# SwiGLU on one core: the first w1 piece issued by three queues, one of them GpSimd's

## The chip, the cores and the metric

The kernel runs on one core of a Trainium2 chip. A core has a matrix engine (TensorE, PE in the profile), a vector engine (VectorE, DVE), an activation engine (ScalarE, ACT), GpSimd (POOL) and a sync engine (SyncE, SP), each with an instruction stream of its own. Loads and stores are started by an instruction on SP, ScalarE or GpSimd and are then moved by the core's 16 DMA engines. Engines wait for each other, and for loads, by semaphores. The metric is the device time of one execution in microseconds; the time of a kernel is the median of its runs.

## The reference

A gated feed-forward block in bf16, with 1024 tokens (32 x 32), D = 512 and F = 1792:

```python
gate = jnp.einsum("bsd,df->bsf", x, w1)
up = jnp.einsum("bsd,df->bsf", x, w3)
h = _silu(gate) * up
out = jnp.einsum("bsf,fd->bsd", h, w2)
```

## The kernel before

**Tiling.** TensorE contracts over the partition axis, 128 at a time. D is 4 slices (index `dt`), F is 14 slices (`fo`), the tokens are 8 tiles of 128 (`nt`) in 2 blocks of 512 (`nb`). gate and up are computed transposed, F on the partitions and tokens along the row, so x is needed transposed (`xT`, D on the partitions). h is kept in that form (`hT`), and serves as the weights of the third product, whose result has the tokens on its partitions and goes out in rows.

**How x gets transposed.** Three quarters of x come in by two transposing loads on SP (lines 78 and 82). The first 256 tokens (tiles 0 and 1, `x_sb`) are loaded as they are, and TensorE transposes them: 8 matmuls of 128 columns against an identity matrix `ident` (`turned`, line 104), copied from PSUM to `xT` by VectorE and ScalarE in turn (`put`, line 114). GpSimd makes `ident` with two instructions of `make_identity`, called on line 51.

**Order.** The schedule is written out by hand: every engine executes its instructions in the order of the code, and semaphores are put in by the framework. TensorE does 6 matmuls on a constant (`keep_warm`, line 92), the 8 transposes, and then the first three F slices (`FK` = 3) for the first 256 tokens: 12 gate matmuls, ordered so that all three slices use `dt` 0, then 1, 2 and 3, and 12 up matmuls in the same order. Then these slices for tokens 256 to 511, whose `xT` comes from the load of line 78. Then the other 11 slices for block 0 and all 14 for block 1, 8 matmuls of 512 columns for each, and last the third product, one token tile after the other. Behind each pair of gate and up banks ScalarE forms the sigmoid (line 131) and VectorE two products (lines 133 and 134).

**Loads.** `load_w` takes the slices `c0` to `c1` of F and `d0` to `d1` of D. The piece that TensorE needs first, w1's first three F slices (384 KB), is split in two halves of 192 KB: `dt` 0 and 1 (used by gate matmuls 1 to 6) and `dt` 2 and 3 (matmuls 7 to 12). Lines 71 to 75 put the loads on two queues. SP issues token tile 0 of x, then the first half of w1's piece; ScalarE issues token tile 1 of x, then a small activation that brings its table in, then the second half. SP goes on with the two halves of w3's first piece, the first transposing load, the larger pieces of w1 and w3, the second transposing load, and all of w2. GpSimd issues no load at all.

Of the kernel before, what the change touches and what calls it, by code (L numbers as in the profile page):

```python
# [10 lines left out]
def kernel(  # L11
# [8 lines left out]
    nc = tc.nc  # L20
# [10 lines left out]
    DT = D // P  # L31
# [7 lines left out]
    w1_v = w1.rearrange("(dt p) f -> p dt f", p=P)  # L39
# [8 lines left out]

    x_view = x_flat.rearrange("(nt p) d -> p nt d", p=P)
    ident = consts.tile([P, P], bf16, name="ident")  # L50
    make_identity(nc, ident[:])
    x_sb = consts.tile([P, HB // P, D], bf16, name="x_sb")
    xT = consts.tile([P, DT, N], bf16, name="xT")
    w1_sb = consts.tile([P, DT, F], bf16, name="w1_sb")
# [4 lines left out]
    FK = 3  # L59

    def load_x(queue, t0, t1):
        queue.dma_start(out=x_sb[:, t0:t1, :], in_=x_view[:, t0:t1, :])  # L62

    def load_w(queue, w_sb, w_v, c0, c1, d0=0, d1=DT):
        f0, f1 = c0 * P, c1 * P
        queue.dma_start(out=w_sb[:, d0:d1, f0:f1], in_=w_v[:, d0:d1, f0:f1])
# [3 lines left out]

    load_x(nc.sync, 0, 1)
    load_x(nc.scalar, 1, 2)
    load_w(nc.sync, w1_sb, w1_v, 0, FK, 0, 2)
    nc.scalar.activation(table[:], one, SIGMOID)  # L74
    load_w(nc.scalar, w1_sb, w1_v, 0, FK, 2, DT)
    load_w(nc.sync, w3_sb, w3_v, 0, FK, 0, 2)
    load_w(nc.sync, w3_sb, w3_v, 0, FK, 2, DT)
    nc.sync.dma_start_transpose(out=xT[:, :, HB:NB], in_=x_flat[HB:NB, :])
# [142 lines left out]
```

## Time and profile before

| | us |
|---|---|
| median of 11 runs | 82.29 |
| fastest and slowest of them | 81.77, 84.26 |
| the profiled execution | 84.38 |
| its span, first to last instruction | 82.6 |
| TensorE busy in the span | 78.2 (95%) |
| VectorE, ScalarE, GpSimd busy | 39.5, 23.4, 0.7 |

The profile is of one execution, and all times in it count from the start of its span. The page's list of groups gives, for each kind of instruction, its line, engine, operation, output and inputs with their shapes, the count, the busy time and the mean of one, and the idle time of the engine ahead of it with what ended that idle time. The timeline gives the same in order of time, with equal neighbours merged: start, length, engine and line, and how many. The chain of waits follows the work that ended last back to the start. A list of DMA issues gives the size of each load and the time from its issue to its landing; PEld is the loading of weights into the array, and a "q" behind an engine's name is its sequencer, which issues the DMAs.

### The profile page before, as it was taken

What the parts mean: (1) busy time and instruction counts of PE and PEld (TensorE: products, weight loads), DVE (VectorE), ACT (ScalarE), POOL (GpSimd) and SP (SyncE); (2) the same over time, 40 slices, a digit from 0 to 9 for tenths busy, and PEclk for the clock granted to TensorE, in tenths of its full rate; (3) what the DMA queues carried; (4) which work ended last, traced back from release to release, by engine and by line L of the source; (5) the groups of instructions that cost most, each with busy time, mean ns of one, the idle gap of its engine ahead of it and who ended that gap; (6) DMA issues with size and microseconds to landing.
All of it is one profiled execution on the core that took longest, in us unless ns stands there. A gap on an engine that the chain in (4) does not pass through costs nothing.

```text
span 82.6 us, 1014 instructions
## 1 busy us (share of the span) xinstructions
PE 78.2 (95%) x382; PEld 38.5 (47%) x388; DVE 39.5 (48%) x60; ACT 23.4 (28%) x40; POOL 0.7 (1%) x6
## 2 busy tenths in 40 slices
PE   6979999999999999999999999999999999999960
PEld 2446784444444444444444444444444444444550
DVE  0130069898788787887878878775000000000010
ACT  4410074224422244222442223430202211220220
POOL 3000000000000000000000000000000000000000
PEclk9999999999999999999999999999999999999999
DMA  1999999999900000000000000000011011011012
GB/s 24 299 253 300 339 349 347 307 229 373 333 29 0 0 0 0 0 0 0 0 12 0 0 0 0 0 4 0 0 64 64 0 64 64 8 64 64 10 54 64
DMA packets 10789, 7.67 MB, mean 93 GB/s; under 512 B 3616, under 2 KB 10784, under 8 KB 10784
## 3 DMA queue, kind: packets, MB, share of 16 engines
q1 hardware_dynamic: 10368, 7.28, 30.4%
q10 hardware_dynamic: 416, 0.33, 1.2%
q8 instruction: 3, 0.05, 0.2%
q14 instruction: 2, 0.02, 0.1%
HBM read 5.77 MB, written 1.05 MB: 83 GB/s over the span
## 4 chain that ended last, share of the span: by engine, by line
PE 90%; DMA 5%; issue 1%; SPq 0%; DVE 0%; DVEq 0%
PE gate_ps L121 31%; PE up_ps L121 30%; PE o_ps L174 29%; DMA w_sb<-in_w_dram 5%; SPq L62 0%; DVE o_sb L183 0%; DVEq L183 0%
## 5 line engine op out<-in xcount | busy, mean ns | idle before, releaser
L121 PEld LDWEIGHTS <-w_sb 128*128 128x128 bf16 x248 | 25.2, 102 | 25.8 <-DMA w_sb<-in_w_dram 0.9
L121 PE MATMUL gate_ps<-xT,w_sb 128*128 128x512 bf16 (+1 forms) x122 | 29.9, 372 | 0.7 <-DMA w_sb<-in_w_dram 0.6
L121 PE MATMUL up_ps<-xT,w_sb 128*128 128x512 bf16 (+1 forms) x122 | 29.5, 368 | 0.1
L131 ACT ACTIVATE sig<-gate_ps 128x512 f32<-128x512 f32 x28 | 16.7, 597 | 34.1 <-PE gate_ps L121 34.1
L133 DVE TENSOR_TENSOR t<-gate_ps,sig 128x512 f32<-128x512 f32 x28 | 19.3, 690 | 11.1 <-ACT sig L131 11.0
L174 PE MATMUL o_ps<-w_sb,hT 128*128 128x512 bf16 (+2 forms) x124 | 24.3, 355 | 0.1
L134 DVE TENSOR_TENSOR hT<-t,up_ps 128x512 bf16<-128x512 f32 x28 | 19.3, 688 | 2.9
L174 PEld LDWEIGHTS <-hT 128*128 128x128 bf16 x126 | 11.8, 98 | 12.7
L183 DVE CAST o_sb<-o_ps 128x128 bf16<-128x128 f32 x1 | 0.3, 291 | 23.0 <-PE o_ps L174 23.0
L185 ACT CAST o_sb<-o_ps 128x512 bf16<-128x512 f32 (+1 forms) x8 | 4.6, 572 | 19.6 <-PE o_ps L174 19.6
L92 PE MATMUL warm_ps<-const-bfloat16-1.0 128*128 128x512 bf16 x6 | 2.7, 623 | 0.8 <-PEq L205 0.8
L114 DVE CAST xT<-pT 128x256 bf16<-128x256 f32 (+1 forms) x3 | 1.1, 380 | 3.8 <-PE pT L104 3.7
L74 ACT ACT_TABLE_LOAD x1 | 1.3, 1283 | 1.2 <-PEq L205 1.2
L92 PEld LDWEIGHTS <-const-bfloat16-1.0 128*128 128x128 bf16 x6 | 0.7, 133 | 1.9 <-issue 1.9
L104 PEld LDWEIGHTS <-x_sb 128*128 128x128 bf16 x8 | 0.8, 135 | 0.8 <-DMA x_sb<-in_x_dram 0.8
L104 PE MATMUL pT<-ident,x_sb 128*128 128x128 bf16 x8 | 1.1, 308 | 0.0
L114 ACT CAST xT<-pT 128x128 bf16<-128x128 f32 (+1 forms) x2 | 0.6, 318 | 1.3 <-PE pT L104 1.3
masks.py:199 POOL TENSOR_SCALAR_AFFINE_SELECT ident<-ident 128x128 bf16<-128x128 bf16 x1 | 0.3, 292 | 0.1
masks.py:197 POOL MEMSET ident<- 128x128 bf16 x1 | 0.2, 204 | 0.3 <-POOLq L205 0.3
L74 ACT ACTIVATE table<-const-bfloat16-1.0 128x1 f32<-128x1 bf16 x1 | 0.2, 203 | 0.0
L205 POOL MEMSET const-bfloat16-1.0<- 128x1 bf16 x1 | 0.1, 102 | 0.0
L205 POOL MEMSET const-uint8-127<- 128x1 uint8 x1 | 0.1, 102 | 0.0
(2 smaller groups left out, 0.2 us busy)
## 6 DMA issues: line engine op xcount, KB each, us to landing
w_sb<-in_w_dram SPq DMA_DIRECT2D x4, 512.0 KB, 7.2
w_sb<-in_w_dram SPq DMA_DIRECT2D x1, 1792.0 KB, 8.4
out_dram<-o_sb SPq DMA_DIRECT2D x7, 128.0 KB, 1.7
w_sb<-in_w_dram SPq DMA_DIRECT2D x2, 384.0 KB, 4.9
w_sb<-in_w_dram SPq DMA_DIRECT2D x3, 192.0 KB, 4.1
w_sb<-in_w_dram ACTq DMA_DIRECT2D x1, 192.0 KB, 4.0
x_sb<-in_x_dram ACTq DMA_DIRECT2D x1, 128.0 KB, 2.7
x_sb<-in_x_dram SPq DMA_DIRECT2D x1, 128.0 KB, 2.6
```

What stands on the lines that cost most here:

```text
L74: nc.scalar.activation(table[:], one, SIGMOID)
L92: nc.tensor.matmul(warm_ps[:, 0:cols], lhsT=one.to_broadcast([P, P]), rhs=one.to_broadcast([P, cols]), start=True, stop=True,)
L104: nc.tensor.matmul(pT[:, i, j, :], lhsT=x_sb[:, nt, dt * P : (dt + 1) * P], rhs=ident[:], start=True, stop=True,)
L114: copy(xT[:, dts[0] : dts[-1] + 1, nts[0] * P : (nts[-1] + 1) * P], pT[:].rearrange("p d t c -> p d (t c)"),)
L121: nc.tensor.matmul(ps[:, c0 : c0 + n1 - n0], lhsT=w_sb[:, dt, fo * P : (fo + 1) * P], rhs=xT[:, dt, n0:n1], start=(dt == 0), stop=(dt == D ...
L131: nc.scalar.activation(sig[:], gate_ps[:], SIGMOID)
L133: nc.vector.tensor_mul(t[:], gate_ps[:], sig[:])
L134: nc.vector.tensor_mul(hT[:, fo, nb * NB : (nb + 1) * NB], t[:], up_ps[:])
L174: nc.tensor.matmul(o_ps[:], lhsT=hT[:, fo, nt * P : (nt + 1) * P], rhs=w2_sb[:, fo, c0 : c0 + DB], start=(fo == 0), stop=(fo == FT - 1),)
L183: nc.vector.tensor_copy(o_sb[:], o_ps[:])
L185: nc.scalar.copy(o_sb[:], o_ps[:])
L205: nc = _bacc.Bacc("TRN2", target_bir_lowering=False, num_devices=1)
```

## The change

The first half of w1's first piece is issued by GpSimd, as its first work, and `make_identity` is called after it. The second half moves from ScalarE's queue to SP's, into the second place there, which the first half has left. ScalarE issues only token tile 1 of x. No load changes its size and no arithmetic changes.

```diff
     ident = consts.tile([P, P], bf16, name="ident")
-    make_identity(nc, ident[:])
...
     load_x(nc.sync, 0, 1)
     load_x(nc.scalar, 1, 2)
-    load_w(nc.sync, w1_sb, w1_v, 0, FK, 0, 2)
+    load_w(nc.gpsimd, w1_sb, w1_v, 0, FK, 0, 2)
+    make_identity(nc, ident[:])
     nc.scalar.activation(table[:], one, SIGMOID)
-    load_w(nc.scalar, w1_sb, w1_v, 0, FK, 2, DT)
+    load_w(nc.sync, w1_sb, w1_v, 0, FK, 2, DT)
     load_w(nc.sync, w3_sb, w3_v, 0, FK, 0, 2)
     load_w(nc.sync, w3_sb, w3_v, 0, FK, 2, DT)
```

## The prediction

> **What bounds the kernel now.** I read the chain of waits first. It is TensorE almost from end to end: the three matmul lines hold 90% of the span. The one thing near the head that isn't TensorE is a transfer:
>
> ```profile
> 0.74 0.39 SPq L62
> 1.13 0.07 issue
> 1.20 3.79 DMA w_sb<-in_w_dram
> 4.99 0.05 issue
> 5.03 2.74 PE gate_ps L121 x12
> 7.78 2.13 PE up_ps L121 x12
> ```
>
> Columns: start, length, what. The first gate matmul starts at 5.03 us because the first half of w1's first piece (192 KB, the load this change hands to GpSimd) was issued on SP at 1.20 and landed at 4.99. All matmuls follow without a hole, so an earlier first gate matmul is worth what it is earlier, and a later one costs the same.
>
> Next the timeline of the first 14 us, for what stands before that wait:
>
> ```profile
> 0.73 0.20 POOL masks.py:197 MEMSET ident<- 128x128 bf16 x1 [0.29 <-POOLq L205]
> 1.01 0.29 POOL masks.py:199 TENSOR_SCALAR_AFFINE_SELECT ident<-ident 128x128 bf16<-128x128 bf16 x1
> 3.35 1.10 PE L104 MATMUL pT<-ident,x_sb 128*128 128x128 bf16 x8
> 5.03 2.74 PE L121 MATMUL gate_ps<-xT,w_sb 128*128 128x256 bf16 x12 [0.59 <-DMA w_sb<-in_w_dram]
> 7.57 2.34 PE L121 MATMUL up_ps<-xT,w_sb 128*128 128x256 bf16 x12
> 9.74 0.60 PE L121 MATMUL gate_ps<-xT,w_sb 128*128 128x256 bf16 x4
> 10.18 0.60 PE L121 MATMUL up_ps<-xT,w_sb 128*128 128x256 bf16 x4
> ```
>
> Three things to see. The identity is ready at 1.30 and first used at 3.35, when x has landed: 2.05 us of cover. TensorE is idle for 0.59 us between the transposes and the gate. And the same 128x256 matmul costs two prices: 12 from 5.03 to 7.57 are 0.212 us each, 4 from 9.74 to 10.18 are 0.11 each. The 12 in between take 2.17 us: n at 0.213 and 12-n at 0.109 gives n = 8.3, so the speed changes at about 9.3 us (the granted clock stands at 1.00 all the while and doesn't show it).
>
> Then the issues and their landing times:
>
> ```profile
> w_sb<-in_w_dram SPq DMA_DIRECT2D x3, 192.0 KB, 4.1
> w_sb<-in_w_dram ACTq DMA_DIRECT2D x1, 192.0 KB, 4.0
> x_sb<-in_x_dram ACTq DMA_DIRECT2D x1, 128.0 KB, 2.7
> x_sb<-in_x_dram SPq DMA_DIRECT2D x1, 128.0 KB, 2.6
> ```
>
> and the stretches of half a microsecond, whose last column is GB/s:
>
> ```profile
> 1.50:2.00 0.50, 0.50 (x2) 0.15 (x1) 0.00 (x0) 0.50 (x1) 0.00 (x0) 1.00 0.47 78
> 2.00:2.50 0.50, 0.50 (x3) 0.21 (x2) 0.00 (x0) 0.49 (x2) 0.00 (x0) 1.00 0.87 248
> 2.50:3.00 0.50, 0.50 (x3) 0.08 (x1) 0.00 (x0) 0.16 (x1) 0.00 (x0) 1.00 0.94 284
> 3.50:4.00 0.50, 0.50 (x6) 0.49 (x6) 0.29 (x1) 0.16 (x1) 0.00 (x0) 1.00 1.07 329
> ```
>
> The first packets move at 1.76, 1.02 us after x's issue began; from 2.0 on the DMA engines move 250 to 330 GB/s. x and both halves of w1's piece are 640 KB and share this. The record of landings adds a detail: 15 of the first half's 16 parts had landed at 4.22, the last at 4.99. One straggling part makes the whole wait of 0.59 us, and no view says why.
>
> **What the skill says.** "DMA: Bandwidth & Descriptors", in "Latency and other measured facts", gives a first byte after about 0.6 us for a load issued by SP or ScalarE and about 1 us for one by GpSimd, whose cores compute the descriptors. The trace agrees on the first: x's issue ends at 1.13, its packets start at 1.76, 0.63 later. It shows no GpSimd load. The same page's "Anatomy of one DMA — SWDGE (gpsimd) path" prices such a load at 2.0 us plus bytes at 436 GB/s. Its "Issuing engines are not separate DMA queues" says that all issuers share 16 engines and interleave; the two queues here do. "TensorE: Matmul & The Clock Gate", Part 1, says that the array runs at half clock until a free-running window of about 3.4 us was busy throughout. The step from 0.213 to 0.109 us at 9.3 fits: the window before its last one, about 2.5 to 5.9, holds the idle 0.59.
>
> **The change, part by part.**
>
> *First w1 half to GpSimd.* It is issued at about 0.72 instead of 1.20, and no longer stands behind x's first 128 KB in SP's queue. Cost by the page's price: 0.72 + 2.0 + 196,608 B / 436 GB/s (0.45) = 3.17, alone on the engines. They aren't idle: if GpSimd needs 1 us for descriptors and the first packet follows 0.63 later, it starts at 2.35. Of x's 262 kB about 125 have moved by then (39 by 2.0, 248 GB/s after). The other 137 kB go at two thirds of some 290 GB/s, 0.71 us, to 3.06. The half has 68 kB then; its other 128 kB go at half of 320 GB/s, 0.80 us, to 3.86, and with the 0.3 us that lie between a load's last packets and its semaphore it lands at about 4.15. Both ends: 3.2 (the bare price) and 5.3 (the slow rival). I take 4.15.
>
> *x* now shares with that half some 0.5 us earlier than before. I put 0 to 0.2 on its landing, 0.15 taken.
>
> *Identity.* Its two instructions (0.73 to 1.30, 0.57 us) now stand behind the DMA on GpSimd: 0.72 + 1.0 + 0.57 = 2.3, still 1 us ahead of x. Cost nothing, hidden by x's landing; the cover is gone if GpSimd holds its DMA for over 2.05 us, and from there each us costs one.
>
> *Second half to SP's second place.* It takes over the issue at 1.20 and that place in the queue, so lands where the first did, 4.99 at the latest. It is needed by the seventh gate matmul, six of 0.213 after the start: 4.40 + 1.28 = 5.68. Hidden. SP's later issues (both w3 halves, the transposing load at 2.67, the big pieces) keep number and place, so they don't move; w3 is needed at 4.40 + 2.56 = 6.96 and its first half lands at 1.66 + 4.1 = 5.8. The transposed second half of x lands at 2.67 + 4.7 = 7.37.
>
> *ScalarE* loses one issue of 0.45 us, beside its table load (1.17 to 2.45). Its next work is a copy at 3.84 that waits for TensorE. Nothing.
>
> *The start of the gate.* The eighth transpose leaves the array 0.107 us after 4.13, at 4.24; with x 0.15 late, 4.39. The w1 half at 4.15 no longer binds. Gain: 5.03 - 4.39 = 0.64 us. What is late next is x itself.
>
> *The clock.* With the hole shut, the window to 5.9 is busy and the fast clock may come one window earlier. Then 3.4 us of matmuls at 0.213 (16) run at 0.109: 16 x 0.104 = 1.66 us more. Total 2.3, just inside the limit of 9.74 - 7.37 = 2.37 which the transposed x sets.
>
> **The sum.** The profiled execution took 84.38: span 82.6 and 1.78 around it. Direct gain: 83.74; with the clock, 82.1. But the median shown is 82.29, 2.09 below that execution. Two readings: the profiled one carries something that lies outside these steps, and the median has the hole too; or most runs have no straggler, no hole and the early clock already (0.6 + 1.7 is just the distance), and there is nothing to win. No view decides. I count the direct 0.64 alone on the median, since an early clock may be in it already: 82.29 - 0.64 = 81.65.
>
> **Rivals.**
>
> *Slower: GpSimd is late.* The price of 1 us for descriptors is for no particular shape. This load has 256 rows of 768 B, so as many reads and writes to be described, and is GpSimd's first. If it holds GpSimd for 2.5 us, the identity is ready at 3.79 and the transposes start 0.45 late; the first packet moves at 3.85, 192 KB at half of 330 GB/s take 1.19, and it lands at 5.04 + 0.3 = 5.34. That is 0.35 later than in the profiled run and 1.1 later than in a run without the straggler; the middle gives 83.0, and a clock window lost with it up to 84.6. It decides from a landing after 4.99, or 4.25 if most runs have no hole. For it: the path isn't seen here, and the half no longer lies in a queue that is already running. Against: the load starts 0.47 us earlier. 0.37.
>
> *No change.* Most runs have the gate waiting only for the transposes, both halves share the bandwidth as before, and the median stays at 82.2. For: the 2.09 us between median and profiled run, and 15 of 16 parts in place at 4.22. Against: the straggler hits three loads in a row, which doesn't look like chance. 0.18.
>
> *Faster by the clock too.* 82.29 - 2.3 = 80.0. Part of the faster case, at 0.12 of its 0.45.
>
> **How the numbers follow.** Faster 0.45: 0.33 around 81.65 (own range 81.2 to 81.9) and 0.12 around 80.2. Within 0.5% (0.41 us, about what a measurement of this kernel can tell from no change) 0.18. Slower 0.37 around 83.0, a quarter of it past 83.7. Leaving about a tenth at each end, the range is 80.3 to 83.7.
>
> **What would show it.** Right: a GpSimd DMA near 0.72 that holds the engine for about 1 us; the identity ready before 2.6; the transposes at 3.35 to 3.5; the first gate matmul at 4.3 to 4.5 with no idle before it that a w1 load ends; the 0.109 us spacing from about 6 or still from 9.3, which sizes the clock's part. Wrong: the first gate matmul after 5.0 still waiting for w1, the transposes waiting for the identity, or w3 or x taking the wait over. If the first gate matmul comes at 4.4 and the median still stands, the second reading of the median was the true one.

## The result and the profile after

The changed kernel takes 85.18 us (median of 12 runs, 83.11 to 85.53) against 82.44 (47 runs, 81.61 to 84.26; the 82.29 above is the median of 11): 2.74 us or 3.3% slower by the medians. The forecast was 0.64 us faster. (The three queues of the title carry x and w1 together. The first w1 piece itself is issued by two, GpSimd's and SP's; ScalarE's has only x.) By the fast runs alone the ratio is only 1.0136 (1.0086 to 1.0186), but the 9 runs above 84.9 that this leaves out belong to the change, as the experiments show, so the medians are the result here.

The profiled execution of the changed kernel took 83.11 us, span 81.3: one of its faster ones. Its chain of waits (start, length, what; only the longest pieces are listed):

```profile
1.25 4.43 DMA w_sb<-in_w_dram
5.73 1.49 PE gate_ps L121 x12
```

The first gate matmul starts at 5.73 instead of 5.03, and waits for the same half of w1 as before, now GpSimd's load. The timeline of the first 14 us:

```profile
1.25 0.83 POOL L65 DMA_DIRECT2D w_sb<-in_w_dram  x1 [0.80 <-POOLq L205]
2.08 0.22 POOL masks.py:197 MEMSET ident<- 128x128 bf16 x1
2.38 0.29 POOL masks.py:199 TENSOR_SCALAR_AFFINE_SELECT ident<-ident 128x128 bf16<-128x128 bf16 x1
3.53 0.97 PE L104 MATMUL pT<-ident,x_sb 128*128 128x128 bf16 x8
5.73 1.49 PE L121 MATMUL gate_ps<-xT,w_sb 128*128 128x256 bf16 x12 [1.24 <-DMA w_sb<-in_w_dram]
7.05 1.47 PE L121 MATMUL up_ps<-xT,w_sb 128*128 128x256 bf16 x12
8.36 0.60 PE L121 MATMUL gate_ps<-xT,w_sb 128*128 128x256 bf16 x4
```

GpSimd's load starts at 1.25, half a microsecond later than the engine's first instruction for the identity before (0.73), and holds it for 0.83 us. The identity is ready at 2.67, well ahead of the transposes. The hole in TensorE's work has grown from 0.59 to 1.24 us. Yet the 12 gate matmuls take only 1.32 us, 0.11 each: this execution has the fast clock by its first gate, where the profile before had slow matmuls to 9.3. The trace also keeps a record of the granted clock. The PEclk column shows 1.00 even where that record has not begun, which is why the prediction saw no change in it; the record itself begins at 9.32 us in the profile before, just where the spacing changes, and at 4.28 here. So the two first profiles are of unlike kinds, and their spans (81.3 and 82.6) must not be compared as they stand.

The issues of the first weight pieces and their landing times:

```profile
w_sb<-in_w_dram SPq DMA_DIRECT2D x3, 192.0 KB, 4.7
w_sb<-in_w_dram POOLq DMA_DIRECT2D x1, 192.0 KB, 4.4
```

GpSimd's load lands 4.4 us after its issue, at 5.69. The three of SP are unlike each other: the record of landings has w1's second half at 3.95, earlier than anything of w1 before, and the two halves of w3 at 6.37 and 6.98, 0.6 later than in the first profile before. Stretches of half a microsecond (last column GB/s) show a low rate in that time:

```profile
3.50:4.00 0.50, 0.47 (x6) 0.47 (x6) 0.14 (x1) 0.04 (x1) 0.00 (x0) 1.00 0.93 171
4.00:4.50 0.50, 0.49 (x6) 0.29 (x3) 0.47 (x2) 0.34 (x2) 0.00 (x0) 1.00 0.78 201
4.50:5.00 0.50, 0.00 (x0) 0.00 (x0) 0.46 (x2) 0.26 (x1) 0.00 (x0) 1.00 0.80 258
```

From 3.5 us the rate falls to 171 and 201 GB/s, where the kernel before moved 329 and 338. I call this the slump.

### The profile page after: what moved, and what is told of

Its sections match the earlier page's. It is cut to its first block, busy times and chain, and to the rows that moved or that the text cites. A ratio compares the mean times of both kernels' runs of the same rounds, so it can differ in the third digit from the quotient of the medians.

```text
span 81.3 us, 1015 instructions
## 1 busy us (share of the span) xinstructions
PE 76.2 (94%) x382; PEld 37.5 (46%) x388; DVE 39.4 (48%) x60; ACT 23.4 (29%) x40; POOL 1.5 (2%) x7
## 4 chain that ended last, share of the span: by engine, by line
PE 89%; DMA 5%; issue 1%; DVE 0%; DVEq 0%; POOLq 0%
PE gate_ps L121 30%; PE o_ps L174 30%; PE up_ps L121 29%; DMA w_sb<-in_w_dram 5%; DVE o_sb L183 0%; DVEq L183 0%; POOLq L205 0%; POOLq masks.py:199 0%
## 5 line engine op out<-in xcount | busy, mean ns | idle before, releaser
L121 PEld LDWEIGHTS <-w_sb 128*128 128x128 bf16 x248 | 24.2, 98 | 25.3 <-DMA w_sb<-in_w_dram 1.4
L121 PE MATMUL gate_ps<-xT,w_sb 128*128 128x512 bf16 (+1 forms) x122 | 28.7, 358 | 1.4 <-DMA w_sb<-in_w_dram 1.2
L121 PE MATMUL up_ps<-xT,w_sb 128*128 128x512 bf16 (+1 forms) x122 | 28.7, 358 | 0.1
L65 POOL DMA_DIRECT2D w_sb<-in_w_dram x1 | 0.8, 828 | 0.8 <-POOLq L205 0.8
```

The costliest lines, as they stand in the source:

```text
L121: nc.tensor.matmul(ps[:, c0 : c0 + n1 - n0], lhsT=w_sb[:, dt, fo * P : (fo + 1) * P], rhs=xT[:, dt, n0:n1], start=(dt == 0), stop=(dt == D ...
```

## The experiments

The theories. A: GpSimd's load lands late, which costs the delay itself, and in most executions the hole it leaves also makes the array stay at half clock (0.213 us for a matmul of 256 columns instead of 0.109) for one more window, as the prediction takes the clock to work. B: only the delay counts; the two levels of time (83.1 to 83.8 and 84.9 to 85.5) have another cause. C: a GpSimd load has a cost of its own, beyond being late. Further letters belong to side questions, and stand in the expectations of the runs.

### What an execution near each median looks like

The kernel before and the changed kernel were profiled again, unchanged.

> The kernel before, unchanged, profiled a second time. Its first profile (84.38 us) had a gate start at 5.03 behind a hole of 0.59 us and slow matmuls to 9.3, but its median is 82.4. Theory A, with the early clock as the usual case: an execution near the median shows matmuls at 0.109 us from some point between 4 and 7.5 us, and the first matmul on the second 256 tokens (the 25th of the gate and up stream) at 7.4 to 8.1 instead of 9.74. Theory B (the first profile is the usual case and 2 us lie outside these steps): spacing 0.213 to 9 us again in an execution of 82.0 to 82.8.

The kernel before took 82.36, near its median. Timeline of TensorE:

```profile
4.44 1.81 PE L121 MATMUL gate_ps<-xT,w_sb 128*128 128x256 bf16 x12
6.09 1.47 PE L121 MATMUL up_ps<-xT,w_sb 128*128 128x256 bf16 x12
7.40 0.60 PE L121 MATMUL gate_ps<-xT,w_sb 128*128 128x256 bf16 x4
```

No idle time is put down ahead of the gate: w1's first half landed at 4.39, as the transposes ended, and no part of it straggled. The spacing drops to 0.11 during the fourth gate matmul (the clock record begins at 5.16), and the second 256 tokens start at 7.40 instead of 9.74. This answers the question that the prediction left, by one execution: near the median there is no hole, and the clock is early. The times agree, since 46 of the 47 runs of the kernel before lie at 82.82 or lower; the first profile was the unusual one. The chain of this execution shows what then binds, a w3 piece (a piece of 0.05 us between the two is left out):

```profile
4.68 6.45 DMA w_sb<-in_w_dram
11.18 1.04 PE up_ps L121 x4
```

TensorE waits about 0.3 us for it at 11.1, so an earlier gate was worth nothing in such an execution.

> The changed kernel, unchanged, profiled a second time. Its first profile (83.11 us) had fast matmuls from the first gate on; most of its runs take 84.9 to 85.5. Theory A: an execution of 84.9 to 85.5 shows the first gate at 5.6 to 6.0, matmuls at 0.213 us from there to 8.5 or later, and the 25th matmul of the gate and up stream at 9.8 to 10.9. Theory B: spacing 0.109 us from the first gate, and the extra 2 us in other places.

> The changed kernel, profiled a third time, in case the second profile is again one with the early clock. Theory A: if 84.9 to 85.5, the slow matmuls last to 8.5 or later; if 83.1 to 83.8, they are over by the first gate. GpSimd's load starts at 1.25 and its first packet moves 2.0 to 2.2 us later in any case.

83.78 and 83.58: neither is of the upper level, and both again have fast matmuls from the first gate on (the clock record begins at 4.88 and 4.50). Their gates start at 6.39 and 6.20, behind holes of 1.67 and 1.55 us, and GpSimd's load lands at 6.35 and 6.15. The first profile's 5.69 was the earliest of the three.

### The hole filled, beside the changed kernel

```diff
+    keep_warm(3, NB)
     gates = [bank("gate_ps", "gate") for _ in range(FK)]
```

> The changed kernel with three more matmuls on the constant between the transposes and the first gate matmul; nothing else. They fill 1.28 us at the slow matmul rate, about the length of the hole (last transpose 4.26, gate 5.73), and add nothing to the path as long as w1 lands after them. Theory A (the hole costs its length and, in most executions, also lets the array stay at half speed for one more window): the matmul spacing drops to 0.109 us by the first gate in nearly all executions, and the median falls from 85.2 to 83.1-83.8. Theory B (only the late gate counts, the two levels of time have another cause): median stays at 85.0 to 85.3. The gate still starts at 5.6 to 5.8 in both.

> The changed kernel, unchanged, timed on the same chip as the next one. Its three profiles so far were all of executions with the early clock (83.11, 83.78, 83.58), while 9 of its 12 timed runs lay at 84.9 to 85.5. Theory A (a hole of 1.2 to 1.7 us makes the clock late in a part of the executions): runs in two groups again, at 83.1 to 83.9 and 84.9 to 85.6, with at least a third in the upper one. Theory B (the upper group belongs to one chip or one moment): all in one group.

> The changed kernel with three matmuls on the constant in the hole, timed again beside the changed kernel. Theory A: nearly no runs in the upper group, median 83.4 to 83.8. Theory B: the same two groups in the same shares as the run beside it.

The changed kernel on this chip: 83.35, 83.61, 84.77, 85.20, 85.44, 85.56, median 84.98. With the filler, on the same chip: 83.45 to 83.80, median 83.56; on another chip 83.18 to 83.78, median 83.70. Above 84.5 lie 13 of the 18 timed runs of the changed kernel and none of the 12 with the filler, though its gate comes no earlier (6.40 and 6.08 in the two profiles, where 5.6 to 5.8 was expected). Two timelines of TensorE show the difference. The changed kernel in its execution of 84.77:

```profile
5.27 2.74 PE L121 MATMUL gate_ps<-xT,w_sb 128*128 128x256 bf16 x12 [0.90 <-DMA w_sb<-in_w_dram]
7.80 2.37 PE L121 MATMUL up_ps<-xT,w_sb 128*128 128x256 bf16 x12
10.01 0.60 PE L121 MATMUL gate_ps<-xT,w_sb 128*128 128x256 bf16 x4
```

and with the filler, 83.80:

```profile
4.45 1.49 PE L92 MATMUL warm_ps<-const-bfloat16-1.0 128*128 128x512 bf16 x3
6.08 1.82 PE L121 MATMUL gate_ps<-xT,w_sb 128*128 128x256 bf16 x12
7.73 1.47 PE L121 MATMUL up_ps<-xT,w_sb 128*128 128x256 bf16 x12
9.04 0.60 PE L121 MATMUL gate_ps<-xT,w_sb 128*128 128x256 bf16 x4
```

The first has its gate 0.8 us earlier than the second (w1 happened to land at 5.22) and still starts the second 256 tokens 1.0 us later, because its slow matmuls (0.21 us apart) last to 9.5, 20 of the 24 gate and up matmuls; with the filler three are slow. The clock record begins at 9.62 in the first and at 6.80 in the second. Filling the hole removes the upper level without an earlier gate: theory B falls, and theory A holds as far as the hole goes.

### A late load without GpSimd

The kernel before, with w1's and w3's first halves exchanged on SP:

```diff
-    load_w(nc.sync, w1_sb, w1_v, 0, FK, 0, 2)
+    load_w(nc.sync, w3_sb, w3_v, 0, FK, 0, 2)
...
-    load_w(nc.sync, w3_sb, w3_v, 0, FK, 0, 2)
+    load_w(nc.sync, w1_sb, w1_v, 0, FK, 0, 2)
```

> The kernel before, with no load on GpSimd, but w1's first half and w3's first half have changed places on SP, so that the first half of w1 is SP's third load. It should land where w3's first half landed, at about 5.8, as late as GpSimd's load. Theory A: a hole of about 1.4 us, gate at 5.8, median 85.0 to 85.5 as in the changed kernel, though GpSimd issues nothing. Theory C (a GpSimd load costs something of its own beyond being late, such as slower DMA engines for the others): under 84, because the other loads run at full rate.

84.62 us (83.01 to 85.17, 6 runs, 5 of them above 84.4), a little under the 85.0 to 85.5 that theory A set; the half landed at 5.42, a little earlier than I had set.

```profile
5.47 2.74 PE L121 MATMUL gate_ps<-xT,w_sb 128*128 128x256 bf16 x12 [0.91 <-DMA w_sb<-in_w_dram]
8.01 1.97 PE L121 MATMUL up_ps<-xT,w_sb 128*128 128x256 bf16 x12
```

A hole and slow matmuls, and a median 0.6 us under the changed kernel's 85.18, with nothing issued by GpSimd and no slump in the DMA rate. The clock's part needs a late load, not a late GpSimd load; theory C isn't needed for it.

### The halves exchanged, and both on SP

First the changed kernel with its two halves exchanged: SP's second load feeds gate matmuls 1 to 6, GpSimd's feeds 7 to 12.

```diff
-    load_w(nc.gpsimd, w1_sb, w1_v, 0, FK, 0, 2)
+    load_w(nc.gpsimd, w1_sb, w1_v, 0, FK, 2, DT)
...
-    load_w(nc.sync, w1_sb, w1_v, 0, FK, 2, DT)
+    load_w(nc.sync, w1_sb, w1_v, 0, FK, 0, 2)
```

> The changed kernel with the two halves exchanged: SP's second load is the first half of w1's piece (gate matmuls 1 to 6), GpSimd issues the second half (matmuls 7 to 12). Theory A: the gate starts at 4.4 and the hole moves behind the sixth matmul, at 5.0 to 5.7 where the array is fast and at most 0.1 us where it is slow; the hole is shorter, so the clock is early in most executions and the median is 82.4 to 83.0. Theory C: still above 83.5.

83.02 us (82.89 to 83.40, 8 runs), ratio 1.0084 (1.0053 to 1.0116) to the kernel before.

```profile
4.37 1.49 PE L121 MATMUL gate_ps<-xT,w_sb 128*128 128x256 bf16 x6
6.03 1.14 PE L121 MATMUL gate_ps<-xT,w_sb 128*128 128x256 bf16 x6 [0.18 <-DMA w_sb<-in_w_dram]
```

With six slow matmuls of work ahead of it, GpSimd's landing at 5.99 costs 0.39 us of idle array (the sixth matmul's 0.213 after 5.43, to 6.03; the timeline's 0.18 counts from the matmul's modelled end) and no run falls into the upper group.

Then the kernel before with ScalarE's half moved to SP, and nothing on GpSimd:

```diff
-    load_w(nc.scalar, w1_sb, w1_v, 0, FK, 2, DT)
+    load_w(nc.sync, w1_sb, w1_v, 0, FK, 2, DT)
```

> Both halves on SP, one behind the other; GpSimd issues nothing and ScalarE only token tile 1 of x. In the changed kernel SP's second load landed at 3.95, so here the first half lands at 3.9 to 4.1 and the second at 4.6 to 4.8, both before they are needed. Theory A: no hole, median 82.2 to 82.5, as the kernel before or a little under it. If the kernel before still loses something to the half that ScalarE issues: 81.7 to 82.0.

82.94 us (82.81 to 83.20), ratio 1.0067 (1.0041 to 1.0094): slower, both expectations missed. The first half landed at 4.00 as expected, the second at 6.01 instead of 4.7, in a slump of its own (stretches as above):

```profile
3.50:4.00 0.50, 0.38 (x4) 0.38 (x5) 0.05 (x1) 0.00 (x0) 0.00 (x0) 1.00 0.77 166
4.00:4.50 0.50, 0.50 (x8) 0.49 (x6) 0.47 (x2) 0.28 (x2) 0.00 (x0) 1.00 1.01 198
```

So the slump needs no load on GpSimd. It comes when ScalarE's half is taken from its queue, which is the other part of the change.

### The slump

The transposing load moved behind the next w1 and w3 pieces, both halves of w1 still on SP:

> Both w1 halves on SP alone (as in the run with SP alone), and the first transposing load moved behind the next pieces of w1 and w3. Theory F (it is the issue of the transposing load, 1.3 us on SP from 3.22 on, that holds up SP's queue): no slump, the second half of w1 lands by 4.7 instead of 6.01 and the DMA rate stays at 300 GB/s or more between 3.5 and 5.0. Theory D (one queue is not enough early on): the rate still falls to 160 to 250 GB/s there and the half lands after 5.5. The time is of no interest here: the transposed x is late and gives 83.5 to 85.

84.9 us in one run; the slump is deeper, 120 and 94 GB/s, and the second half lands at 5.89. Theory F (the issue of the transposing load holds up SP's queue) falls.

```profile
3.50:4.00 0.50, 0.27 (x3) 0.28 (x4) 0.00 (x0) 0.00 (x0) 0.00 (x0) 1.00 0.76 120
4.00:4.50 0.50, 0.50 (x8) 0.49 (x6) 0.42 (x2) 0.27 (x1) 0.00 (x0) 1.00 0.50 94
```

All of w1's piece as one load of 384 KB, SP's second, so that ScalarE issues only x and GpSimd nothing:

```diff
-    load_w(nc.sync, w1_sb, w1_v, 0, FK, 0, 2)
+    load_w(nc.sync, w1_sb, w1_v, 0, FK)
...
-    load_w(nc.scalar, w1_sb, w1_v, 0, FK, 2, DT)
```

> All 384 KB of w1's first piece as one load, SP's second; ScalarE only token tile 1 of x, GpSimd nothing. Theory K (SP's third load is slow to start whoever else issues, and shows as a slump only where SP's second load has run out by 3.5 us): the second load lasts to 4.5, so no slump, 300 GB/s or more between 3.5 and 5.0, w3's halves at 5.5 and 6.1, the transposed x at 6.9. Theory D (one queue alone is not enough early on): 160 to 250 GB/s there, w3's halves at 6.4 and 7.0. The gate waits for all of w1, landing at 4.9 to 5.1 (5.9 by theory D), a hole of 0.6 us, so the median is 82.3 to 84.5 either way.

No slump:

```profile
3.50:4.00 0.50, 0.50 (x6) 0.50 (x6) 0.29 (x1) 0.17 (x1) 0.00 (x0) 1.00 1.03 330
4.00:4.50 0.50, 0.43 (x5) 0.17 (x2) 0.45 (x2) 0.34 (x2) 0.00 (x0) 1.00 1.10 341
```

82.49 us (82.18 to 85.04, 20 runs, 4 of them above 84.4), ratio 1.0023 (0.9999 to 1.0047). One queue alone can fill the DMA engines at that time, so theory D (one queue isn't enough early on) falls as it was put. What fits all profiles is theory K, put a little wider: the slump comes where SP's second load has run out by about 3.5 us and its third has to follow, with no load left in ScalarE's queue (in the changed kernel GpSimd's load is under way beside it). Why the third starts so slowly isn't shown. The transposed x landed at 7.31, not 6.9.

Two queues used more, the second half of w3 on ScalarE too:

```diff
     load_w(nc.scalar, w1_sb, w1_v, 0, FK, 2, DT)
+    load_w(nc.scalar, w3_sb, w3_v, 0, FK, 2, DT)
...
-    load_w(nc.sync, w3_sb, w3_v, 0, FK, 2, DT)
```

> The kernel before, with the second half of w3's first piece moved from SP to ScalarE, behind ScalarE's half of w1. SP then issues the transposing load half a microsecond earlier (2.2 instead of 2.67). Theory D (early in the kernel the DMA engines run at 330 GB/s only while two queues hold loads, and slump to half with SP's alone): no slump, w3 and the transposed x land at 6.2 and 6.9 instead of 6.4 and 7.37, median 82.0 to 82.3. Theory E (the number of queues doesn't matter, the bytes do): 82.3 to 82.5, no change.

82.38 us (81.92 to 84.81, 14 runs, 2 of them above 84.5), ratio 1.0016 (0.9978 to 1.0054): no change; the transposed x landed at 7.42. And w1's piece split 1 to 3 between ScalarE and SP:

```diff
-    load_w(nc.sync, w1_sb, w1_v, 0, FK, 0, 2)
+    load_w(nc.sync, w1_sb, w1_v, 0, FK, 1, DT)
...
-    load_w(nc.scalar, w1_sb, w1_v, 0, FK, 2, DT)
+    load_w(nc.scalar, w1_sb, w1_v, 0, FK, 0, 1)
```

> The kernel before with the same two queues, but w1's first piece split 1 to 3: ScalarE issues slice dt 0 (96 KB, gate matmuls 1 to 3), SP's second load is dt 1 to 3 (288 KB). If the DMA rate holds (as in the run where GpSimd had the small slice and SP the large one) the small slice lands at 3.9 to 4.1 and the large one at 4.5 to 4.7, the gate starts at 4.3 to 4.4 with at most 0.3 us of idle in it, and the transposed x lands at 6.9: median 81.7 to 82.1, faster than the kernel before. If the first three gate matmuls only move the hole to the fourth, or the transposed x still lands at 7.4: 82.3 to 82.6.

82.36 us (81.84 to 84.36, 14 runs, 1 of them above 84), ratio 1.0005 (0.9974 to 1.0036): no gain. No kernel of this study beats the one before. The w3 piece at 11.1 us is the limit in one profile alone; in the profiles of the last three kernels the gate itself still waits for w1 (0.88, 0.52 and 1.08 us).

### What GpSimd's load costs

The identity made first, the load behind it:

```diff
-    load_w(nc.gpsimd, w1_sb, w1_v, 0, FK, 0, 2)
     make_identity(nc, ident[:])
+    load_w(nc.gpsimd, w1_sb, w1_v, 0, FK, 0, 2)
```

> The changed kernel with the identity made before GpSimd's load instead of after it. Theory G (the 0.5 us between GpSimd's release at 0.7 and the recorded start of its load at 1.25 are set-up of the load itself): the load starts 0.5 us after the identity's last instruction, at about 1.8, and lands at 6.0 to 6.4. Theory H (GpSimd's sequencer is simply released late for any first instruction but the identity's, or the set-up runs beside other work): it starts at 1.3 to 1.4 and lands at 5.7.

83.83 us in one run. Timeline of GpSimd:

```profile
1.02 0.29 POOL masks.py:199 TENSOR_SCALAR_AFFINE_SELECT ident<-ident 128x128 bf16<-128x128 bf16 x1
1.45 0.83 POOL L65 DMA_DIRECT2D w_sb<-in_w_dram  x1
```

The load starts 0.14 us after the identity and only 0.2 later than in the changed kernel: most of the 0.5 us ahead of the load passes beside the identity's work (the start is nearly that of theory H). In its place at the head it gains 0.2 us, not the 0.6 of the identity's length. It landed at 6.42 here, not at theory H's 5.7; the unchanged load landed anywhere from 5.22 to 6.35, so one landing says little.

Half the rows for GpSimd, the other three slices as SP's second load:

```diff
-    load_w(nc.gpsimd, w1_sb, w1_v, 0, FK, 0, 2)
+    load_w(nc.gpsimd, w1_sb, w1_v, 0, FK, 0, 1)
...
-    load_w(nc.sync, w1_sb, w1_v, 0, FK, 2, DT)
+    load_w(nc.sync, w1_sb, w1_v, 0, FK, 1, DT)
```

> GpSimd loads one slice of w1 (dt 0, 128 rows, 96 KB) instead of two; SP's second load takes the other three (288 KB). Theory I (GpSimd's cost goes by rows): it holds GpSimd for 0.4 to 0.5 us instead of 0.83, and its first packet moves 0.4 us sooner, at 2.9. Theory J (fixed cost): 0.8 us and 3.2 to 3.3. In both its landing is earlier than 5.69, since it is half the bytes: 4.6 to 5.2.

> The kernel of the run with GpSimd loading 128 rows, timed. Its gate started at 4.86, half a microsecond after the transposes, and its transposed x landed at 6.91, earlier than in the kernel before. Theory A: a hole of 0.5 us costs less than 0.5 us here, and lets the clock be late in some executions only: median 82.5 to 83.3, lower than the changed kernel's 85.2, although GpSimd still issues the first weights that TensorE needs. If it is GpSimd's part in the start as such that costs: 84 or more.

```profile
1.25 0.67 POOL L65 DMA_DIRECT2D w_sb<-in_w_dram  x1 [0.80 <-POOLq L205]
```

128 rows hold GpSimd for 0.67 us, 256 for 0.83: mostly fixed (an estimate from these two: 0.51, and 0.16 for each 128 rows). The first packet moved at 3.51, no sooner than with 256 rows. The load landed at 4.81 and 5.42 in two profiles; there was no slump (396 and 363 GB/s in the first where the changed kernel has 171 and 201). Timed: 82.60 us (82.14 to 84.81, 20 runs, 2 of them above 84), ratio 1.0026 (1.0001 to 1.0050). So GpSimd can issue the first weights at hardly a loss if its load is small and SP's second is long; in the changed kernel both are 192 KB.

This run also limits theory A. Its second profile has a hole of 0.98 us, like the exchanged halves of w3 and w1 (0.91), which had 5 of 6 runs in the upper group. The share of late clocks doesn't follow from the length of the hole alone. The clock record shows what is missing: when the full clock came. 16 of the 18 profiles have such a record, and they fall into three groups.

| the record begins at, us | profiles | idle of TensorE |
|---|---|---|
| 3.81 to 4.88 | 6, among them three of the changed kernel and the second one of this run | the hole comes later, or is at most 0.4 us old |
| 5.16 to 6.80 | 6, among them both with the filler and the kernel before at 82.36 | the timeline puts down at most 0.23 between the first warm-up matmul and the full clock |
| 8.81 to 9.62 | 4: the kernel before at 84.38, the changed kernel at 84.77, the exchanged halves of w3 and w1, the split 1 to 3 | a hole of 0.59 to 1.08 ahead of it |

So a hole was harmless to the clock where the full clock came before it or soon after it began; behind a hole of 0.59 us or more that it had not come before, it came only at 8.8 to 9.6. What sets that time in an execution isn't shown, and why the shares differ (2 of 20 here) stays open, as one or two profiles don't give the holes of the other runs.

## Why the prediction was wrong

**The sum, in one relation.** In the profiles of the changed kernel, time minus the start of the second 256 tokens is 83.11 - 8.36 = 74.75, 83.78 - 9.03 = 74.75, 83.58 - 8.83 = 74.75 and 84.77 - 10.01 = 74.76. All behind that point is the same; the change acts on the first 10 us only. In the execution of the kernel before near its median the point is at 7.40, and 74.96 follow, with the wait for w3 in them. The lower group of the changed kernel has its middle at 83.55, 1.1 above the kernel before: the late gate, with fast matmuls behind it. The upper group, 13 of 18 runs, has its middle at 85.30, another 1.75 above. The filler and the one profile from that group put this on the clock. The prediction had priced one window of clock at 1.66.

**Step that failed first: GpSimd's load.** It was to land at 4.15 and landed at 5.69 in the first profile, between 5.2 and 6.4 in all. Three terms of that step, each read too low: the issue begins at 1.25, not 0.72 (0.53 us); from there to the first packet, at 3.29, it takes 2.04 us, not 1.63 (0.41); and from there to the semaphore 2.40, not 1.80 (0.60), in the time in which the rate fell to half. The sum, 1.54, is the whole miss of the landing. The prediction's own sign of being wrong came true with it: the first gate matmul after 5.0, still waiting for w1. The page of the Trainium skill, "DMA: Bandwidth & Descriptors", in "Latency and other measured facts", states a first byte after about 1 us. Counted from the end of the issue, 2.08, it is 1.21 us here, so the figure is about right, but the time that the load holds GpSimd, 0.83, and the start-up ahead of it, 0.5, come on top. I had taken the 1 us for the holding and added SP's 0.63. The fixed price of 2.0 us plus bytes in "Anatomy of one DMA — SWDGE (gpsimd) path" gives an estimate of 2.45 from issue to landing; 4.0 to 5.1 were measured beside the other loads.

**SP's later issues were not to move, and ScalarE's lost load was to cost nothing.** In the first profiles the w3 halves and the transposed x land 0.6 us later than before (6.37, 6.98, 8.01). Over all profiles the first w3 half lands at 5.30 and 5.78 before and at 5.67 to 6.82 after, so mostly later. ScalarE's half was what kept the DMA engines busy between 3.5 and 4.5 in this order of loads. The same page's "Issuing engines are not separate DMA queues" says that issuing from several engines saves only the issue time. With both halves on SP the second was issued 0.45 us later (1.68 for 1.23), but landed at 6.01, 0.77 and 1.29 later than in the two profiles of the kernel before (5.24, 4.72). That is more than the issue time; the measurement decides.

**The median.** The prediction named two readings of the 2.09 us between median and profiled run and put the gain on the median as if the hole were in it. The second reading was true: 82.36 us is an execution without hole and with the early clock. In such an execution there was nothing to gain, whatever GpSimd did; the late landing then made it a loss.

**The slower rival** had the right outcome and the right threshold (a landing after 4.25 if most runs have no hole), even the clock window (83.0, with it 84.6), at 0.37 and not as the forecast. Its reason was wrong: it had GpSimd held for 2.5 us by the descriptors, with the identity late; it was held for 0.83, and the identity was ready 0.9 us early. The delay lies ahead of the issue and behind it, so its landing of 5.34 came near the measured 5.2 to 6.4 in part by luck.

**What held.** The identity is hidden. x shares with the weights and its transposes start 0.18 us later (0.15 taken). The second half of w1 landed at 3.95, inside 4.99. The clock's price was right in size (1.66 for 1.75), but with the sign turned round.

## What to carry to other kernels

A profile of one execution must be placed in the spread of the runs before anything is priced against it: here the wait that the change was to remove wasn't in the median at all, and two spacings of the same matmul in the profile said why. A gap in TensorE's work during the first microseconds can cost more than its length: here 13 of 18 runs lay 1.75 us above the rest, and in the one of them that was profiled the slow matmuls lasted to 9.6 us. Three matmuls on a constant in the gap took that part back. The first load that TensorE waits for did better on SP's queue, whose first packet moved 1.0 us after the issue, than on GpSimd's (2.0 to 2.2). What another queue carries beside it may be what keeps the DMA engines busy, as ScalarE's half did here.

## What was not expected of the hardware

- A GpSimd load of 192 KB, first on its engine: 0.5 us of start-up, 0.83 us of holding the engine (0.67 for half the rows), the first packet 2.0 to 2.2 us after the issue starts (2.3 for half the rows), landing 4.0 to 5.1 us after it. SP's first load: 0.39 us and 1.0 us to the first packet.
- Most of the start-up of a GpSimd load ran beside its other work: with the identity ahead of it the load started only 0.2 us later (one run).
- The full clock came at 3.8 to 6.8 us or, behind a hole of 0.59 us or more, at 8.8 to 9.6, in executions of one kernel too (5.16 and 9.32 for the kernel before).
- Early in the kernel, between 3.5 and 4.5 us, the DMA engines moved 88 to 257 GB/s (by half microseconds) in each profile where SP's second load was 192 KB and ScalarE had no weights to load, and 272 to 396 where either was otherwise. The cause is open.
